# Relative-position attention and a sine-activated feed-forward on one core: bias bands from TensorE instead of a DRAM bounce, another load order, and a staged key transpose for the second batch

## The chip, the cores and the metric

The kernel runs on one NeuronCore of a Trainium2 chip. The metric is device time in microseconds (us) of one execution; before the change it is 374.09 us, the median of 3 runs (373.94 to 374.35).

## The reference

Eight batches, eight heads, 576 positions, head size 64. Attention with a bias that depends only on the distance of two positions, then a feed-forward with a sine:

```
scores = q @ k.T / 8 ; scores += bias_table[bucket(|i - j|)]     # 32 buckets, one value for each head
attn   = softmax(scores) ; x = attn @ v                          # x: 4608 x 512, heads side by side
h = x @ w_in ; g = h + sin(alpha*h)**2 / alpha ; out = g @ w_out # 512 -> 2048 -> 512
```

Every distance of 128 or more falls into the last bucket, so the bias differs from that bucket's value only in a band around the diagonal. The kernel subtracts the last bucket's value from the table (which softmax does not feel), takes the exponential of the rest, and multiplies the exponentials of the scores by this factor inside the band alone.

## The kernel before, in words

One Python planner (`Plan`, L61) holds some thousands of tasks, each with a cost, dependencies, a priority and an earliest time, and writes the instructions of all engines in one fixed order. The planner's times leave no trace in the program except through that order: each engine runs its own list from top to bottom and waits on semaphores.

Work goes by batch `t` (8 of them). For a batch: scores by TensorE (PE) in units of 128 keys x 512 queries x 2 heads into PSUM (L682 to L706), exponentials by ScalarE (ACT, L723), band multiplications by VectorE (DVE, L754), products with v on PE (`plan_av`, L973), a normalization on DVE (L967, L968), and a transpose into `xT`. The feed-forward of block `b` follows: `w_in` products (L1078), sine and some squares on ACT (L1083, L1090), other squares and the sum on DVE (L1092, L1097), and `w_out` products (L1139 to L1142) which the planner lays into gaps of PE's work, mostly during the next batch's attention. All matrix products come from the helper `full` at L478, so in the profile they share that line and are told apart by their tiles.

The first batch is loaded as fp32 or cast by the queue of GpSimd (POOL), and its keys and queries are transposed on PE, head pair by head pair (`plan_tr`, L564, matmuls at L573 and L579), copied out of PSUM by DVE (L562). The second batch's keys and queries come in natural order too (tile `nat2`, `load_nat2`, L542) and are transposed on PE in the middle of block 0's feed-forward. From batch 2 on, POOL writes fp16 copies to DRAM (`staged_k`, `staged_q`, L405), and the queue of SyncE (SP) turns them on the way back with DMA transposes (L412). GpSimd copies the last 64 keys of each head into `kt` (L416, L599).

The band factors: the table difference is made with a matmul of `less_last` and the table `tabN` (L613), its exponential is `tabE` (L616); a product with the one-hot constant `phi_sb` spreads it over 512 distances (`e_sb`, L622, L625). It is written five times to DRAM (`e_dram`, L626) and read back by SP with a stride of one element from partition to partition, into `m2r` and `mhr` (L492, L499, L630 to L633). Six of the eight loads of the first batch's v (`load_v32`) stand behind these reads in SP's list.

POOL's queue in the first 50 us: natural-order keys and queries of batch 0, casts of v, `w_in` in three pieces (L459), `nat2` keys then queries (L454), `w_out` in four pieces (L464), v of batch 1 (L424, L448), then the staging of batch 2 (L407). PE's fillers (`warm1`, L484, tile `zz`) are matmuls without a use that the planner writes where it sees a gap in the first 26 us.

`HEAD_PRI` (L255) is a table by hand or search: it gives the priorities of the first tasks by number.

Of the kernel before, what the change touches and what calls it, by code (L numbers as in the profile page):

```python
# [10 lines left out]
F16 = mybir.dt.float16  # L11
# [26 lines left out]
BANKS = {"h": (0, 1, 2, 3, 4, 5), "av": (6, 7), "mo": (7, 6)}  # L38

# [21 lines left out]
class Plan:  # L61
# [86 lines left out]
    def run(self, t0):  # L148
        free = dict(t0)
        todo = list(self.tasks)  # L150
        while todo:
# [21 lines left out]
            for e, c in cands.items():  # L173
# [5 lines left out]
                fin = st + t.engs[e]  # L179
# [34 lines left out]
T_START = {"PE": 4.25, "ACT": 5.2, "DVE": 5.05, "POOL": 5.5, "SP": 5.0}  # L214
SPLIT = {0: 3, 1: 3}
PRI_S = 0
T_WI = 16.4
T_TAB = 4.9
T_PHI = 5.4
T_CL = 9.6  # L220
T_FIRST = (4.3, 5.35)
T_PAIR = ((7.05, 8.1), (8.9, 10.6), (12.5, 13.4))
PRI_TR = (350, 950, 1250)
T_VT = 9.7
T_ACT = ()
T_M2 = (12.4, 14.6, 16.0, 16.0)
T_MH = 13.5
T_RST = 20.0
T_WL = 25.0
T_V0 = (6.5, 8.8, 16.4, 16.9, 17.4, 17.9, 18.4, 18.9)  # L230
T_P3 = 8.3
# [5 lines left out]
T_LD = 33.0  # L237
# [4 lines left out]
SQ = {"ACT": 0.52, "DVE": 0.38}  # L242
T_V = ((15.0, 15.0), (53.5, 53.5))
T_TR1 = (35.5, 39.0)
T_W = (24.2, 27.0, 33.0, 33.0)
T_WO = (42.0, 45.0, 47.8, 51.0)
WARM0 = 7
WARM1 = 0
# [18 lines left out]
}  # L267
SIN_SET = "trig_and_small"
SLACK = {"PE": 0.02, "ACT": 0.02, "DVE": 0.02, "POOL": 0.02, "SP": 0.02}
# [14 lines left out]
def kernel(  # L284
# [26 lines left out]
    NE = 5  # L311
# [8 lines left out]
    e_dram = nc.dram_tensor("e_dram", [NE, 4 * H, EW], F16, kind="Internal")  # L320
# [5 lines left out]
    last_np = np.eye(NB, dtype=np.float32)  # L326
    last_np[NB - 1] -= 1.0
    phi_h = nc.inline_tensor(phi_np, "phi_const")
    last_h = nc.inline_tensor(last_np, "last_const")
# [8 lines left out]
    m2r = sgl.tile([128, H, XW], F16, name="m2r")  # L338
    mhr = sgl.tile([128, NP, 192], F16, name="mhr")
    m2 = m2r[:, :, ::-1]  # L340
    mh = mhr[:, :, ::-1]
# [12 lines left out]
    tabN = sgl.tile([NB, H], F32, name="tabN")  # L354
    tabE = sgl.tile([NB, H], F16, name="tabE")
    phi_sb = sgl.tile([NB, EW], F16, name="phi_sb")
    less_last = sgl.tile([NB, NB], F32, name="less_last")
    e_sb = sgl.tile([H, EW], F16, name="e_sb")
    alphaN = sgl.tile([NF, 128], F32, name="alphaN")
    idf_sb = sgl.tile([NF, NF], F32, name="idf_sb")  # L360
# [886 lines left out]
```

## Time and profile before

| | |
|---|---|
| median of the runs | 374.09 us |
| profiled execution, first to last instruction | 372.5 us |
| what the runs' median has beside that span | 1.6 us |
| PE, ACT, DVE, POOL busy | 363.7, 318.3, 258.8, 89.2 us |
| start of the first score exponential | 9.39 us |
| start of the long stretch of `w_in` products of block 0 | 31.19 us |
| first score product of batch 1 | 51.49 us |

The profile gives only the span of the profiled execution, not a separate time for it. PE's busy time counts matmuls from issue to their modelled end, so neighbours overlap, and a stretch with full busy time need not be at the highest rate. "PEclk" is the granted clock of TensorE. An engine's list is in order, so one waiting instruction holds all behind it.

### The profile page before, as it was taken

The numbers are of one execution on the slowest core, as the hardware profiler recorded it, in microseconds if no ns is written. First come the engines' busy times: TensorE is split into PE (matmuls) and PEld (weight loads), VectorE is DVE, ScalarE is ACT, GpSimd is POOL, SyncE is SP. The second block draws the span as 40 slices with busy tenths as digits, with TensorE's granted clock in tenths as the row PEclk, the third lists the DMA queues.
The fourth block names the chain that finished last, engine by engine and source line by source line (L and its number), as shares of the span: only waits on it lengthen the run. The fifth ranks groups of instructions, "written<-read, shape, count | busy, mean of one in ns | idle before, by whom it ended". The sixth has DMA issues, their size and how long they took to land.

```text
span 372.5 us, 8907 instructions
## 1 busy us (share of the span) xinstructions
PE 363.7 (98%) x3563; PEld 195.3 (52%) x3563; DVE 258.8 (69%) x555; ACT 318.3 (85%) x436; POOL 89.2 (24%) x130
## 2 busy tenths in 40 slices
PE   6989989999999999999999999999999999999996
PEld 2455445644465445784554456444676455444443
DVE  4697966678776967597659866787669675879100
ACT  2898999989998999799989999899979997999211
POOL 5575360065000730064003700090006000000000
PEclk9599999999999999999999999999999999999999
DMA  9799999299824996199917992699249121000122
GB/s 167 152 191 208 203 170 155 61 146 123 113 60 99 115 151 112 48 161 138 135 48 135 126 169 59 115 114 171 60 111 118 65 58 48 7 18 13 59 85 84
DMA packets 149690, 40.69 MB, mean 109 GB/s; under 512 B 137144, under 2 KB 144656, under 8 KB 149648
## 3 DMA queue, kind: packets, MB, share of 16 engines
q0 software_dynamic: 94928, 17.47, 58.1%
q1 hardware_dynamic: 54352, 22.30, 25.5%
q8 instruction: 28, 0.46, 0.5%
q10 hardware_dynamic: 368, 0.34, 0.3%
q14 instruction: 14, 0.11, 0.1%
HBM read 37.73 MB, written 16.56 MB: 146 GB/s over the span
## 4 chain that ended last, share of the span: by engine, by line
PE 87%; DVE 4%; DMA 3%; ACT 3%; issue 1%; SPq 0%; ACTq 0%; DVEq 0%
PE pb L478 86%; DVE g L1097 1%; DMA tabN<-in_bias_table_dram 1%; DVE u L754 1%; DMA m2r<-e_dram 1%; DMA e_dram<-e_sb 1%; ACT sq L1090 1%; PE pb L1039 1%; ACT s L1083 1%; ACT nat L723 1%; DVE sq L1092 0%; DVE kT L562 0%; ACT L1161 0%; SPq L501 0%; DVE xn L968 0%
## 5 line engine op out<-in xcount | busy, mean ns | idle before, releaser
L723 ACT ACTIVATE u<-pb 128x1024 f16<-128x1024 f32 (+1 forms) x146 | 137.6, 1015 | 8.8 <-PE pb L478 7.4
L478 PE MATMUL pb<-w_out,g 128*128 128x512 f16 (+2 forms) x592 | 138.7, 374 | 0.5 <-DVE kT L562 0.5
L478 PE MATMUL pb<-xT,w_in 128*128 128x512 f16 (+4 forms) x704 | 127.5, 340 | 0.0
L1097 DVE SCALAR_TENSOR_TENSOR g<-sq,inv_a,pb 128x512 f16<-128x512 f16 x144 | 101.1, 743 | 7.7 <-ACT sq L1090 3.8
L1083 ACT ACTIVATE s<-pb,alphaT 128x512 f16<-128x512 f32 x144 | 92.9, 692 | 11.1 <-PE pb L478 10.2
L478 PEld LDWEIGHTS <-w_in 128*128 128x128 f16 x704 | 64.6, 98 | 57.1
L754 DVE TENSOR_TENSOR u<-u,m2r 128x768 f16<-128x768 f16 (+1 forms) x128 | 63.2, 498 | 35.6 <-ACT u L723 33.7
L478 PEld LDWEIGHTS <-g 128*128 128x128 f16 x592 | 54.0, 98 | 60.3 <-issue 5.4
L478 PEld LDWEIGHTS <-u 128*128 128x128 f16 x1152 | 43.1, 97 | 10.9 <-issue 5.8
L1090 ACT ACTIVATE sq<-s 128x512 f16<-128x512 f16 x75 | 46.8, 637 | 1.2 <-DVE g L1097 0.3
L419 POOL COPY kt<-kT 64x256 f16<-64x256 f16 x12 | 5.1, 428 | 174.2 <-DMA kT<-staged_k 144.9
L478 PE MATMUL pb<-qT,kT 64*128 64x64 f16 (+1 forms) x512 | 44.0, 293 | 1.6 <-ACT u L723 0.6
L478 PE MATMUL pb<-v,u 128*128 128x65 f16 x1024 | 43.7, 193 | 0.0
L1092 DVE TENSOR_TENSOR sq<-s 128x512 f16<-128x512 f16 x69 | 28.8, 427 | 12.1 <-ACT s L1083 11.2
L968 DVE TENSOR_TENSOR xn<-pb,rd 128x256 f16<-128x256 f32 (+2 forms) x59 | 28.5, 483 | 2.0
L478 PEld LDWEIGHTS <-kT 64*128 64x128 f16 x512 | 16.3, 95 | 23.1 <-issue 16.2
L478 PE MATMUL pb<-vh,u 128*128 128x130 f16 x128 | 28.3, 221 | 0.0
L424 POOL DMA_DIRECT2D v<-in_v_dram x28 | 24.8, 898 | 6.9 <-DMA w_in<-in_moe_w_in_dram 2.6
L560 ACT ACTIVATE outs<-pb 128x512 f32<-128x512 f32 (+2 forms) x10 | 5.5, 554 | 19.9 <-PE pb L478 19.9
L562 DVE COPY outs<-pb 128x512 f32<-128x512 f32 x27 | 18.5, 686 | 3.8 <-PE pb L478 3.8
L1161 ACT ACT_TABLE_LOAD x15 | 19.2, 1283 | 0.3
L967 DVE RECIPROCAL rd<-pb 128x4 f32<-128x4 f32 (+2 forms) x59 | 11.0, 186 | 10.8 <-PE pb L478 10.7
(74 smaller groups left out, 181.2 us busy)
## 6 DMA issues: line engine op xcount, KB each, us to landing
out_dram<-outs SPq DMA_DIRECT2D x35, 256.0 KB, 2.3
v<-in_v_dram POOLq DMA_DIRECT2D x28, 128.0 KB, 5.1
staged_k<-in_k_dram POOLq DMA_DIRECT2D x6, 576.0 KB, 9.6
staged_q<-in_q_dram POOLq DMA_DIRECT2D x6, 576.0 KB, 12.0
w_out<-in_moe_w_out_dram POOLq DMA_DIRECT2D x4, 512.0 KB, 17.4
w_out<-in_v_dram SPq DMA_DIRECT2D x8, 128.0 KB, 5.2
w_in<-in_moe_w_in_dram POOLq DMA_DIRECT2D x2, 512.0 KB, 6.3
w_in<-in_moe_w_in_dram POOLq DMA_DIRECT2D x1, 1024.0 KB, 11.6
```

The source lines that it names most:

```text
L424: nc.gpsimd.dma_start(out=vs[t % 2][:, c, :, 0:D], in_=vp[128 * c : 128 * c + 128],)
L478: nc.tensor.matmul(out=out, lhsT=lhsT, rhs=rhs, start=start, stop=stop)
L562: k_of(e).tensor_copy(out=o, in_=i)
L723: nc.scalar.activation(out=o, in_=x, func=AF.Exp, scale=0.125)
L754: nc.vector.tensor_tensor(out=io, in0=io, in1=m2[:, 2 * p : 2 * p + 2, x0 : x0 + hi - lo], op=ALU.mult)
L967: nc.vector.reciprocal(out=r, in_=x[:, :, :, D])
L968: nc.vector.tensor_tensor(out=xn[:, 0:n].rearrange("p c (z d) -> p c z d", z=2), in0=x[:, :, :, 0:D], in1=r.unsqueeze(3).to_broadcast([128 ...
L1083: nc.scalar.activation(out=s16.v, in_=h.v, func=AF.Sin, scale=alphaT[:, f : f + 1])
L1090: nc.scalar.activation(out=sq.v, in_=s16.v, func=AF.Square)
L1092: k_of(e).tensor_tensor(out=sq.v, in0=s16.v, in1=s16.v, op=ALU.mult)
L1097: nc.vector.scalar_tensor_tensor(out=gcell[b].v[:, f, :], in0=sq.v, scalar=inv_a[:, f : f + 1], in1=h.v, op0=ALU.mult, op1=ALU.add,)
L1161: nc.scalar.preload_act_table_set(name)
```

## The change

It has five parts.

1. **Bands on TensorE.** `phi` becomes a 128 x 512 constant: four copies of the one-hot table, each shifted by one distance, and four mask columns. `less_last` (now made on DVE from an identity) gives the table on all four partition groups; DVE spreads it into `tab4` (32 columns: head by shift). For each third of a band, 32 matmuls with a sliding 128-column window of `phi_sb` as stationary operand and `tab4` as moving operand (128 x 32 each) fill two PSUM banks, and one copy by ACT or DVE puts 128 x 8 x 128 values into `m2`. `mh` is copied from `m2`. `e_sb`, `e_dram` and its reads go.
2. **Bias table first.** `tabN` is POOL's first DMA instead of ACT's fourth; `phi_sb` goes from SP's queue to ACT's.
3. **v of batch 0 and `w_in` earlier.** All eight v loads follow each other in SP's list; the `w_in` loads stand in POOL's list after the first v cast.
4. **Keys of batch 1 staged.** They are written to `staged_k` by POOL and turned by an SP DMA transpose; `kt` is copied from there by DVE. The queries still come as `nat2` and over PE.
5. **New order.** The planner gets a DMA "engine" with sizes for each load, a slower PE between two times (`COLD`), other costs, and 250 new entries of `HEAD_PRI`. Tasks of block 0 depend on modelled loads instead of fixed times.

Cut to its core:

```diff
-LAT = {"PE": 0.2, "ACT": 0.18, "DVE": 0.18, "POOL": 0.2, "SP": 2.4}
+LAT = {"PE": 0.2, "ACT": 0.18, "DVE": 0.18, "POOL": 0.2, "SP": 2.4, "DMA": 1.9}
...
+T_START = {"PE": 4.25, "ACT": 5.2, "DVE": 5.05, "POOL": 6.7, "SP": 9.0, "DMA": 13.3}
+STAGED = (0,)
+COLD = (8.4, 14.0, 1.2)
 HEAD_PRI = {
+    0: 5620.10946, 1: 10120.37866, 2: 5619.629986, 3: 10068.1594, 4: 10068.68213, 5: 5620.024503, 6: 5620.936454, 7: 10068.51148, 8: 5619.947209, 9: 10069.00727,
...
-    phi_np = np.zeros((NB, EW), dtype=np.float16)
-    for x in range(EW - 1):
-        phi_np[bt[abs(x - 255)], x] = 1.0
+    phi_np = np.zeros((NJ * NB, EW), dtype=np.float16)
+    for j in range(NJ):
+        for x in range(EW - NJ):
+            phi_np[NB * j + bt[abs(x - 252 - j)], x] = 1.0
+        phi_np[NB * j : NB * j + NB, EW - NJ + j] = 1.0
...
+    def stage(t, kq):
+        dst, src = ((staged_k, k), (staged_q, q))[kq]
+        nc.gpsimd.dma_start(
+            out=dst.ap()[t].rearrange("s (h d) -> s h d", h=H),
+            in_=src[t].rearrange("h s d -> s h d"),
+        )
...
+    P_.dma_start(out=tabN, in_=bias_table)
     P_.memset(id_sb, 1.0)
...
-    nc.scalar.dma_start(out=less_last, in_=last_h.ap())
-    nc.scalar.dma_start(out=tabN, in_=bias_table)
-    nc.sync.dma_start(out=phi_sb, in_=phi_h.ap())
+    nc.scalar.dma_start(out=phi_sb, in_=phi_h.ap())
     nc.sync.dma_start(out=alphaN, in_=moe_alpha.rearrange("(f p) -> f p", p=128))
     load_v32(0)
     load_v32(1)
     load_vt32()
+    for h in range(2, H):
+        load_v32(h)
...
+        def spread(e):
+            nc.vector.tensor_tensor(
+                out=tab4, in0=tabE.unsqueeze(2).to_broadcast([NJ * NB, H, NJ]),
+                in1=phi_sb[:, EW - NJ : EW].unsqueeze(1).to_broadcast([NJ * NB, H, NJ]), op=ALU.mult,
+            )
...
+        tab = plan.add({"DVE": 0.12}, spread, [x], -3000, nb=T_PHI)
+        n = XW // 3
+        for k, w in enumerate((1, 2, 0)):
+            b = Buf("sc")
+            def mm(e, b=b, w=w):
+                o = bank(b, 2).rearrange("p k x -> p (k x)")
+                for i in range(n // NJ):
+                    x0 = EW - NJ - 128 - n * w - NJ * i
+                    full(o[:, NJ * H * i : NJ * H * (i + 1)], phi_sb[:, x0 : x0 + 128],
+                         tab4.rearrange("p h j -> p (h j)"), True, True)
+            def cp(e, b=b, w=w):
+                copy_on(e, m2[:, :, n * w : n * (w + 1)].rearrange("p h (i j) -> p h i j", j=NJ),
+                        bank(b, 2).rearrange("p k x -> p (k x)").rearrange("p (i h j) -> p h i j", h=H, j=NJ))
+            x = plan.add({"PE": BAND_PE}, mm, [tab], -1100 + 10 * k, new=[b])
+            bands[w] = plan.add({"ACT": 0.95, "DVE": 1.15}, cp, [x], -1100 + 10 * k, use=[b])
...
+    def load(eng, cost, emit, size, pri, deps=(), after=(), nb=0.0):
+        x = plan.add({eng: cost}, lambda e: emit(), deps, pri, nb, after=after)
...
+        return x, plan.add({"DMA": size}, lambda e: None, [y], pri)
...
+        for kq in range(2):
+            if kq in STAGED:
+                pool("kq%d" % kq, (2.3, 2.6)[kq], lambda kq=kq: stage(1, kq), (4.4, 5.0)[kq])
+            else:
+                pool("kq%d" % kq, 0.8, lambda kq=kq: load_nat2(kq), 3.1)
...
-                for kq in range(2):
-                    tr[(1, p, kq)] = plan_tr(1, p, kq, 10085 + 20 * p, T_TR1[kq])
+            for kq in range(2):
+                y = [loads["%s%d" % ("t" if kq in STAGED else "kq", kq)][1]]
+                if kq in STAGED:
+                    z = []
+                    if kq == 0:
+                        z = [plan.add({"DVE": 0.35}, lambda e: load_kt(1, nc.vector), y, 10080)]
+                    for p in range(NP):
+                        tr[(1, p, kq)] = y, z
+                    continue
+                for p in range(NP):
+                    tr[(1, p, kq)] = plan_tr(1, p, kq, 10085 + 20 * p, 0.0, y)
```

The change moves instructions at three places that matter below.

POOL's list around the loads of batch 1 and of the weights, before (`w_in`, `nat` with buffer 95 is `nat2`):

```order
L459 DMA w_in_78<-in_moe_w_in_dram 128x4x1024
L740 TENSOR_TENSOR u<-u,mhr 128x128
L444 CAST v_72<-w_out_79 128x4x64 x3
L454 DMA nat_95<-in_k_dram 96x8x384
L454 DMA nat_95<-in_q_dram 96x8x384
L740 TENSOR_TENSOR u<-u,mhr 128x128
L464 DMA w_out_79<-in_moe_w_out_dram 128x4x512 x4
L424 DMA v_73<-in_v_dram 128x8x64 x4
L448 DMA vh_75<-in_v_dram 64x4x64 x2
```

The same place after the change (the last `w_in` load stands 12 rows above the first row):

```order
L809 TENSOR_TENSOR u<-u,mh 128x128
L616 COPY kt_70<-kT_66 64x64 x2
L422 DMA staged_k<-in_k_dram 4608x1x64
L616 COPY kt_70<-kT_66 64x64 x2
L482 DMA nat_95<-in_q_dram 96x8x384
L809 TENSOR_TENSOR u<-u,mh 128x128
L491 DMA w_out_79<-in_moe_w_out_dram 128x4x512 x3
L809 TENSOR_TENSOR u<-u,mh 128x128
L491 DMA w_out_79<-in_moe_w_out_dram 128x4x512
L448 DMA v_73<-in_v_dram 128x8x64 x4
```

The staging of batch 1's keys now stands between `w_in` and the `nat2` queries, in the same queue.

PE's list where block 0's `w_in` products become dense, before (`xn` is the normalized attention output, turned into `xT`):

```order
L478 MATMUL pb<-xT,w_in_78 128x512
L1039 LDWEIGHTS xn
L1039 MATMUL pb<-id_sb,xn 128x128
...
L478 LDWEIGHTS w_in_78
L478 MATMUL pb<-xT,w_in_78 128x512
```

The same place after:

```order
L505 MATMUL pb<-xT,w_in_78 128x512
L593 LDWEIGHTS nat_95
L593 MATMUL pb<-id_sb,nat_95 64x96
...
L1109 LDWEIGHTS xn
L1109 MATMUL pb<-id_sb,xn 128x128
...
L593 LDWEIGHTS nat_95
L593 MATMUL pb<-id_sb,nat_95 64x96
...
L505 LDWEIGHTS w_in_78
L505 MATMUL pb<-xT,w_in_78 128x512
```

Two of the four transposes of batch 1's queries (12 matmuls each) have moved from between the dense products to ahead of them, one of them ahead of the last turn of `xn`.

ACT's list at the start of the score exponentials, before (`u` holds exponentials of scores):

```order
L616 ACTIVATE tabE<-pb 32x8
L625 ACTIVATE e_sb<-pb 8x512
L626 DMA e_dram<-e_sb 8x5x512
L723 ACTIVATE u<-pb 128x2x512 x3
L723 ACTIVATE u<-pb 128x512
```

After (`m_76` is the band table `m2`):

```order
L630 ACTIVATE tabE<-pb 128x8
L574 ACTIVATE m_76<-pb 128x8x128
L791 ACTIVATE u<-pb 128x2x512 x3
L791 ACTIVATE u<-pb 128x512
L791 ACTIVATE u<-pb 128x2x512
L574 ACTIVATE m_76<-pb 128x8x128
```

Two band copies stand in ACT's list where `e_sb` stood; the third is on DVE.

More of the change, by code (lines that the diff above doesn't have):

```diff
@@ L241 @@
 NORM0 = 1200
[L242 to L246, printed above, removed]
+SQ = {"ACT": 0.53, "DVE": 0.41}
 WARM0 = 7
+COLD = (8.4, 14.0, 1.2)
 WARM1 = 0
@@ L310 @@
     EW = 512
-    NE = 5
+    NJ = 4
     ctx.enter_context(tc.manual_schedule())
@@ L512 @@
     )
+    P_.tensor_copy(out=idf_sb, in_=id_sb[0:NB, 0:NB])
     for kq, src in ((0, k), (1, q)):
@@ L608, in plan_table @@
     def plan_table():
-        a, b = Buf("h"), Buf("h")
+        a = Buf("h")
         def less(e):
-            full(bank(a)[0:NB, 0:H], less_last, tabN, True, True)
+            full(bank(a)[:, 0:H], less_last.rearrange("a j b -> a (j b)"), tabN, True, True)
         def ex(e):
-            nc.scalar.activation(out=tabE, in_=bank(a)[0:NB, 0:H], func=AF.Exp)
-        x = plan.add({"PE": 0.15}, less, [], -1200, nb=T_TAB, new=[a])
-        x = plan.add({"ACT": 0.15}, ex, [x], -1200, use=[a])
-        def mm(e):
-            full(bank(b)[0:H, 0:EW], tabE, phi_sb, True, True)
@@ L742, in bd @@
                 )
-            d = plan.add({"POOL": 0.6} if t == 0 and p else {"DVE": 0.25 if two else 0.15}, bd, [x],
-                         base + 10, nb=late, use=[ub])
+            d = plan.add({"POOL": 0.6} if t == 0 and p else {"DVE": 0.25 if two else 0.15}, bd, [x] + band,
+                         base + 10, use=[ub])
             for pp in (p, p + 1) if two else (p,):
```

229 lines of the change are left out of this document (120 added, 109 removed), and 35 rows, old and new, of the table HEAD_PRI.

## Prediction

> **What bounds the kernel now.** I read the page's busy times and its chain first.
>
> ```profile
> PE 363.7 (98%) x3563; PEld 195.3 (52%) x3563; DVE 258.8 (69%) x555; ACT 318.3 (85%) x436; POOL 89.2 (24%) x130
> PE 87%; DVE 4%; DMA 3%; ACT 3%; issue 1%; SPq 0%; ACTq 0%; DVEq 0%
> ```
>
> TensorE is busy 98% of the span and holds 87% of the chain. The chain in order of time and the busy times by stretch tell where it does not:
>
> ```profile
> 2.22 4.77 DMA tabN<-in_bias_table_dram
> ...
> 8.81 3.42 DMA e_dram<-e_sb
> ...
> 13.96 4.43 DMA m2r<-e_dram
> ...
> 75.86 37.92 PE pb L478 x358
> 60.00:360.00 300.00, 300.00 (x2891) 161.96 (x2890) 215.35 (x457) 266.03 (x361) 57.22 (x64) 1.00 0.78 96
> ```
>
> In the first 20 us the chain hangs on the bias table's load, the bounce and the read back. From 60 to 360 us PE has no idle time. So a change early in the program counts only by how much sooner PE comes to its long dense work, and by what PE no longer has to do after that. PE's timeline around that point (start, length, operation, idle before):
>
> ```profile
> 30.32 0.28 PE L1039 MATMUL pb<-id_sb,xn 128*128 128x128 f16 x2
> ...
> 31.19 8.36 PE L478 MATMUL pb<-xT,w_in 128*128 128x512 f16 x38
> 39.48 0.70 PE L579 MATMUL pb<-id_sb,nat 96*64 96x96 f16 x24
> 40.12 1.90 PE L478 MATMUL pb<-xT,w_in 128*128 128x512 f16 x8
> 41.95 0.45 PE L579 MATMUL pb<-id_sb,nat 96*64 96x96 f16 x12
> 42.33 1.04 PE L478 MATMUL pb<-xT,w_in 128*128 128x512 f16 x4
> ...
> 47.00 0.45 PE L579 MATMUL pb<-id_sb,nat 96*64 96x96 f16 x12 [0.31 <-ACT qT L560]
> 47.91 0.59 PE L478 MATMUL pb<-w_out,g 128*128 128x512 f16 x2 [0.47 <-DVE kT L562]
> ...
> 52.40 0.67 PE L478 MATMUL pb<-qT,kT 64*128 64x512 f16 x4 [0.52 <-ACT nat L723]
> ```
>
> I call the start of the 38 products P; it is 31.19. Behind P, PE works to the end with only three short waits, 0.31 + 0.47 + 0.52 = 1.30 us.
>
> **The work behind P.** Of the eight transposes of batch 1, the four of the keys go away (a DMA turns them) and two of the queries move ahead of P, so six of 12 matmuls leave this stretch. By the starts above 12 take 42.33 - 41.95 = 0.38 and 24 take 40.12 - 39.48 = 0.64; at 0.37 each, six are 2.2 us. The waits of 0.31 and 0.47 end with copies of kT and qT on ACT and DVE, of which half are gone. The remaining copies and the squares still keep both engines nearly as full as PE, so I leave 0.5 of the 1.30 us and count 0.8 gained; the bounds are 0 and 1.3. The `w_out` products only change places: 13 more of them come ahead of batch 1's first score product and as many fewer after. So, if P' is the new P, the span is P' + (372.5 - 31.19) - 2.2 - 0.8 = P' + 338.3.
>
> **The head up to the end of batch 0's attention.** Its parts, with the half-clock stretch, are in these rows (PE, ACT, and the granted clock as the third number from the end in the stretches):
>
> ```profile
> 7.12 0.20 PE L478 MATMUL pb<-tabN,less_last 32*32 32x8 f32 x2 [1.94 <-DMA tabN<-in_bias_table_dram]
> 9.28 0.69 PE L579 MATMUL pb<-id_sb,nat 96*64 96x96 f16 x12
> 9.90 0.61 PE L478 MATMUL pb<-qT,kT 64*128 64x512 f16 x2
> ...
> 9.39 2.18 ACT L723 ACTIVATE u<-pb 128x1024 f16<-128x1024 f32 x2 [0.61 <-PE pb L478]
> 24.68 1.03 ACT L723 ACTIVATE u<-pb 128x1024 f16<-128x1024 f32 x1
> 26.30 2.43 ACT L723 ACTIVATE u<-pb 128x1024 f16<-128x1024 f32 x3 [0.59 <-PE pb L478]
> 5.17 0.76 DVE L562 COPY kT<-pb 128x576 f16<-128x576 f16 x1
> ...
> 8.00:8.50 0.50, 0.50 (x7) 0.42 (x6) 0.50 (x1) 0.31 (x1) 0.00 (x0) 0.73 1.22 233
> 18.50:19.00 0.50, 0.50 (x5) 0.19 (x3) 0.50 (x1) 0.50 (x1) 0.37 (x1) 1.00 1.20 313
> ```
>
> The 1.94 us in which PE waited for the bias table, with the first query transposes queued behind it, go away. The band needs 96 matmuls of 32 columns, which the trace does not show. The nearest rows are 12 transposes of 96 columns: 0.38/12 = 32 ns at full clock, (9.90 - 9.28)/12 = 52 ns at half clock. Below lies zero; I take the two rows, 1.0 or 1.65 us for 32. ACT gets two band copies of the exponential's shape (1024 elements from PSUM, 1.03 us in the row) and loses `e_sb`. The first copy must precede the first exponential. With `tab4` at about 6.5 (an estimate: behind the key copy on DVE, which ends at 5.93, and the load of `phi`, four times larger than before), band matmuls to 7.6 and the copy to about 8.75, the first exponential comes at 8.75 instead of 9.39. Then ACT pays a second copy (1.0) and waits about 2 us for bands two and three on PE at half clock, against 0.61 + 0.59 and some smaller waits before. The exponentials ended at 26.30 + 2.43 = 28.73; mine end at 28.8, between 27.2 (clock never falls) and 30. DVE gains the band tables 3 to 10 us earlier, and pays about 2 us for a cast and two copies in time where it was idle. So **the attention of batch 0 ends about when it did**, and PE could take up the dense products at about 31.5, between 30 and 32.7.
>
> **The load that comes last.** Ahead of them PE now has the `nat2` query transposes. When do the queries land? First, the order in which POOL's queue finishes. POOL's own timeline shows it, since it waits for old transfers before it issues more:
>
> ```profile
> 25.32 0.83 POOL L454 DMA_DIRECT2D nat<-in_k_dram  x1
> 35.02 0.88 POOL L424 DMA_DIRECT2D v<-in_v_dram  x1 [2.64 <-DMA w_in<-in_moe_w_in_dram]
> 38.00 0.87 POOL L424 DMA_DIRECT2D v<-in_v_dram  x1 [2.10 <-DMA nat<-in_k_dram]
> 40.84 0.87 POOL L424 DMA_DIRECT2D v<-in_v_dram  x1 [1.97 <-DMA nat<-in_q_dram]
> 43.36 0.63 POOL L448 DMA_DIRECT2D vh<-in_v_dram  x1 [1.65 <-DMA w_out<-in_moe_w_out_dram]
> ```
>
> `w_in`, keys, queries, `w_out` end in the order of issue, each about 2.6 to 3 us after the one before. After the change `staged_k` stands ahead of the queries, so they land behind it. Rates, by stretch (the last number is GB/s), and the sizes of one transfer, with its time to landing:
>
> ```profile
> 12.00:12.50 0.50, 0.50 (x10) 0.24 (x6) 0.16 (x1) 0.50 (x1) 0.26 (x1) 0.50 0.00 0
> 30.00:40.00 10.00, 10.00 (x72) 4.76 (x69) 7.67 (x16) 9.00 (x16) 4.14 (x6) 1.00 1.25 206
> 91.00:91.50 0.50, 0.50 (x4) 0.24 (x3) 0.50 (x2) 0.50 (x1) 0.00 (x0) 1.00 2.43 155
> ...
> staged_k<-in_k_dram POOLq DMA_DIRECT2D x6, 576.0 KB, 9.6
> w_out<-in_v_dram SPq DMA_DIRECT2D x8, 128.0 KB, 5.2
> w_in<-in_moe_w_in_dram POOLq DMA_DIRECT2D x1, 1024.0 KB, 11.6
> phi_sb<-phi_const SPq DMA_DIRECT2D x1, 32.0 KB, 3.5
> ```
>
> At 12.0 all that was issued early had moved; the queue was empty. The changed program moves the same by then, and further, without a pause: six more v loads (6 x 131 KB at about 270 GB/s, an estimate under the 313 of the stretch at 18.50, when v was what moved: 2.9 us), three more quarters of `phi` (98 KB, 0.4), `w_in` (2.1 MB at 206 GB/s, 10.2), `staged_k` (590 KB at 155, the rate of the staging at 91 us: 3.8), the queries (590 KB at 206: 2.9). That is 20.2 us, so 32.2; the queue is not full just before 12.0 (0.8 less) and landing takes some tenths (0.8 more). POOL issues `staged_k` at about 20, behind a copy of batch 0's keys, which is well before `w_in` has moved. I take 32.2, with 30.5 (all at the best rates) and 34.5 (the key transposes take their share, below) as ends. This is later than the 30.3 at which PE gets there: **PE waits about 2 us for the queries**, with the last `xn` turn and all of block 0's products queued behind. Then come two transposes and a turn, 0.37 + 0.11 + 0.37, and a hand-over of 0.1: P' = 33.2.
>
> **Sum.** 33.2 + 338.3 = 371.5 span; with the 1.6 us that the median of the runs has beside the profiled span, **373.1 us**, 1.0 below 374.1. What the head wins or loses by about 1 us is hidden by the wait; if the wait goes, the end of the attention is next (31.5), and the full gain appears.
>
> **Two rules of the Trainium skill** bear on this wait. A PE gap of 1.94 us was followed by half clock from about 8.2 to 18.5 in the rows above, and the seven `zz` matmuls of the start took 0.45 us each, twice the 0.22 of the 38 products:
>
> ```profile
> 1.27 3.17 PE L478 MATMUL pb<-zz 128*128 128x512 f16 x7 [1.27 <-DVE zz L532]
> ```
>
> The Trainium skill, "TensorE: Matmul & The Clock Gate", Part 1, has the half clock come after an idle window of about 3.4 us. By that, a wait of 2 us costs nothing more and the sum stays 373.1; the trace disagrees, since less idle time was enough, so a rival below carries it. The Trainium skill, "DMA: Bandwidth & Descriptors", Queues, rings and completion order, lets each DMA engine go round its queues packet by packet. By that, the turning of batch 1's keys on SP's queue, which starts when `staged_k` has landed, would take half of the engines from the queries, up to 1.4 us: 374.5. No row of before shows the two together.
>
> **Rivals.**
> - *No wait*: loads at their best rates, or the attention ends late enough. P' = 30.7 to 32.3, middle 31.6: 371.5. For it: the early stretch moved up to 313 GB/s. Against: the cast loads moved 206 GB/s in the row of 30 to 40 us. Chance 0.20.
> - *The wait trips the clock* (slower): as at 7.12, PE idles about 2 us, the granted clock halves, and the dense products take 0.43 instead of 0.22 each. The price is 1.6 us if the clock comes back after 3.2 us, as after the `zz` row, and up to 5 us if after 10 as in the mixed work of 8 to 18. Near the first: 374.7 to 376. It decides from a gap of about 1.9 us on. Against: work around this gap is denser than around the first. Chance 0.22.
> - *The head is later than the load*: `phi` lands late, or half-clock bands starve ACT; the attention ends 3 us later, P' = 34.6: 374.5 to 376. Chance 0.08.
> - *The change moves no bound*: the gain behind P is eaten by ACT and DVE, 374.1. Chance 0.05.
>
> **Numbers.** The forecast, 372.2 to 374.2 with 373.1 in its middle, has 0.45. A measurement of this kernel tells about 0.2% (0.75 us) from no change. Faster than that: two thirds of the forecast (0.30) and the first rival (0.20), 0.50. Within: 0.10 of the forecast, 0.05 of the clock's rival, 0.05 of the last, 0.20. Slower: 0.05, 0.17 and 0.08, 0.30. The range 370.4 to 376.2 leaves out the deepest case on each side.
>
> **What would show it.** In the new profile: PE's wait at the query transposes (`nat`), with the DMA of `nat` as releaser, of about 2 us; `staged_k` landing ahead of it at 29 to 30; dense products from 33; no waits on `m2`; the clock at 1.00 behind the wait. If the transposes start without a wait, the DMA sum is wrong; if the exponentials end after 31, the head's sum is.

## The result, and the profile after

The changed kernel takes **383.81 us** (median of 4 runs, 383.74 to 383.93) beside 374.01 us for the kernel before on the same chip: a ratio of 1.0244, 95% interval 1.0207 to 1.0282. It is 9.8 us slower. The forecast was 373.1 us, between 370.4 and 376.2: a small gain, where there is a clear loss.

The profiled execution has a span of 382.1 us, 9.6 more than before. The page's busy times, PE's busy tenths in 40 equal slices of the span, and the granted clock in the same slices:

```profile
PE 364.3 (95%) x3607; PEld 196.8 (51%) x3607; DVE 260.1 (68%) x563; ACT 316.2 (83%) x432; POOL 89.0 (23%) x123
...
PE   8539999999999999999999999999999999999996
...
PEclk9858999999999999999999999999999999999999
```

PE has as much to do as before (364.3 against 363.7 us) and does it in 95% of the span instead of 98%. So the loss is idle time. The row of PE puts it into slices 2 and 3, about 10 to 29 us, and the clock is low there and in slice 4. PE's own timeline (start, length, operation, idle time before it and what ended it):

```profile
6.57 0.95 PE L505 MATMUL pb<-tab,phi_sb 128*128 128x32 f16 x32
...
17.70 0.61 PE L505 MATMUL pb<-qT,kt 128*128 128x256 f16 x2 [3.92 <-POOL kt L616]
27.55 0.60 PE L505 MATMUL pb<-v,u 128*128 128x65 f16 x8 [6.14 <-POOL v L472]
40.88 0.45 PE L593 MATMUL pb<-id_sb,nat 96*64 96x96 f16 x12 [0.50 <-DMA nat<-in_q_dram]
41.85 4.06 PE L505 MATMUL pb<-xT,w_in 128*128 128x512 f16 x18
```

The dense `w_in` products start at 41.85 instead of 31.19: that is 10.66 us, more than the whole loss. Ahead of them PE waits 3.92 us for a `kt` copy and 6.14 us for a cast of v, both on POOL. The wait for the queries, on which the prediction turned, is 0.50 us. POOL's timeline shows why the copy and the cast were late:

```profile
7.86 2.25 POOL L487 DMA_DIRECT2D w_in<-in_moe_w_in_dram  x3
...
16.42 0.56 POOL L472 CAST v<-w_out 128x256 f16<-128x256 f32 x1 [2.73 <-DMA w_out<-in_v_dram]
16.93 0.71 POOL L616 COPY kt<-kT 64x64 f16<-64x64 f16 x2
19.95 0.40 POOL L472 CAST v<-w_out 128x256 f16<-128x256 f32 x1 [2.31 <-DMA w_out<-in_v_dram]
25.45 0.40 POOL L472 CAST v<-w_out 128x256 f16<-128x256 f32 x1 [5.10 <-DMA w_out<-in_v_dram]
26.41 1.09 POOL L472 CAST v<-w_out 128x256 f16<-128x256 f32 x3 [0.56 <-DMA w_out<-in_v_dram]
...
28.31 2.21 POOL L422 DMA_DIRECT2D staged_k<-in_k_dram  x1
31.02 0.79 POOL L482 DMA_DIRECT2D nat<-in_q_dram  x1
```

Read it from top to bottom, since POOL works its list in order. The casts wait for the fp32 loads of v (tile `w_out`, where they are parked). Behind each cast stands what PE needs: the copy of `kt` at 16.93, which ends the 3.92 us; the cast of head 0, last of all, which ends the 6.14 us, since the first product with v needs heads 0 and 1; and then the staged keys at 28.31 and the queries at 31.02. The loads of v were issued by 10.8 us, and this is how long they took (the line of the v loads, all eight; the `w_in` loads below it):

```profile
DMA to landing us min/median/max: 3.9/8.3/16.5
...
w_in<-in_moe_w_in_dram POOLq DMA_DIRECT2D x2, 512.0 KB, 10.5
w_in<-in_moe_w_in_dram POOLq DMA_DIRECT2D x1, 1024.0 KB, 16.8
```

Before, the slowest v load took 6.1 us. Now it takes 16.5: it runs beside 2.1 MB of `w_in`. The busy times by stretch show what that does (PE first, then the granted clock, the DMA share and GB/s as the last three numbers):

```profile
15.00:20.00 5.00, 2.30 (x20) 1.06 (x21) 2.25 (x5) 1.67 (x3) 1.21 (x4) 0.54 1.21 199
20.00:25.00 5.00, 1.15 (x5) 0.24 (x3) 1.23 (x2) 2.36 (x3) 0.35 (x1) 0.50 1.08 197
25.00:30.00 5.00, 2.45 (x28) 1.79 (x28) 1.23 (x4) 0.71 (x1) 3.94 (x8) 0.50 0.03 5
30.00:35.00 5.00, 5.00 (x81) 3.71 (x78) 3.63 (x12) 4.16 (x7) 4.41 (x8) 0.75 1.49 96
```

From 15 to 25 the DMA engines are full and every compute engine is idle half of the time or more; from 25 to 30 the DMA engines have nothing to do (5 GB/s), because the next loads have not been issued: POOL, which issues them, has been waiting for the previous ones. PE works at half clock from about 18 to 32.

### The profile page after: what moved, and what is told of

Its sections match the earlier page's. It is cut to its first block, busy times and chain, and to the rows that moved or that the text cites. A ratio compares the mean times of both kernels' runs of the same rounds, so it can differ in the third digit from the quotient of the medians.

```text
span 382.1 us, 8960 instructions
## 1 busy us (share of the span) xinstructions
PE 364.3 (95%) x3607; PEld 196.8 (51%) x3607; DVE 260.1 (68%) x563; ACT 316.2 (83%) x432; POOL 89.0 (23%) x123
## 4 chain that ended last, share of the span: by engine, by line
PE 88%; DMA 8%; SPq 2%; ACT 1%; POOL 0%; DVE 0%; issue 0%; ACTq 0%; POOLq 0%
PE pb L505 87%; DMA w_out<-in_v_dram 4%; DMA nat<-in_q_dram 3%; SPq L459 1%; DMA natx<-in_k_dram 1%; ACT u L791 1%; PE pb L1109 0%; PE pb L593 0%; SPq L464 0%; POOL v L472 0%; DVE outs L576 0%; DVE u L823 0%; ACT xT L574 0%; ACT outs L574 0%; POOL kt L616 0%
## 5 line engine op out<-in xcount | busy, mean ns | idle before, releaser
L823 DVE TENSOR_TENSOR u<-u,m 128x768 f16<-128x768 f16 (+1 forms) x128 | 61.8, 489 | 34.0 <-ACT u L791 32.1
L505 PEld LDWEIGHTS <-u 128*128 128x128 f16 x1152 | 44.8, 99 | 17.1 <-issue 11.5
L505 PE MATMUL pb<-v,u 128*128 128x65 f16 x1024 | 45.2, 196 | 6.2 <-POOL v L472 6.1
L1160 ACT ACTIVATE sq<-s 128x512 f16<-128x512 f16 x80 | 49.5, 637 | 1.8 <-DVE g L1167 1.0
L505 PE MATMUL pb<-qT,kT 64*128 64x64 f16 (+1 forms) x512 | 42.4, 291 | 0.4 <-ACT u L791 0.3
L1162 DVE TENSOR_TENSOR sq<-s 128x512 f16<-128x512 f16 x64 | 26.9, 424 | 15.4 <-ACT s L1153 14.8
L505 PEld LDWEIGHTS <-kT 64*128 64x128 f16 x512 | 15.5, 95 | 22.9 <-issue 16.4
L576 DVE COPY outs<-pb 128x512 f32<-128x512 f32 x29 | 19.9, 687 | 2.2 <-PE pb L505 1.7
L574 ACT ACTIVATE outs<-pb 128x512 f32<-128x512 f32 (+2 forms) x8 | 4.3, 544 | 19.8 <-PE pb L505 19.8
```

The source lines that it names most:

```text
L505: nc.tensor.matmul(out=out, lhsT=lhsT, rhs=rhs, start=start, stop=stop)
L576: k_of(e).tensor_copy(out=o, in_=i)
L823: nc.vector.tensor_tensor(out=io, in0=io, in1=m2[:, 2 * p : 2 * p + 2, x0 : x0 + hi - lo], op=ALU.mult)
L1160: nc.scalar.activation(out=sq.v, in_=s16.v, func=AF.Square)
L1162: k_of(e).tensor_tensor(out=sq.v, in0=s16.v, in1=s16.v, op=ALU.mult)
```

## The experiments

Most of these kernels differ from the changed kernel, or from the one before, only in the place of a few steps on POOL. `e6`, `e7` and `e9` also give the planner new dependencies, `e12` and `e14` make one copy on another engine, and `e10` and `e13` turn the keys of batch 1 on TensorE, with new dependencies as well. The planner still makes its whole plan; a table `MOVED` then says behind which task others are written into the program. The common edit (`e1` to `e14`; it shifts line numbers by 7):

```diff
+MOVED = {17: [26, 28, 30]}
...
+        self.nth = list(self.tasks)
+        self.index = {t: i for i, t in enumerate(self.nth)}
...
-            t.emit(e)
+            i = self.index[t]
+            if not any(i in x for x in MOVED.values()):
+                t.emit(e)
+            for j in MOVED.get(i, ()):
+                self.nth[j].emit("POOL")
```

In the changed kernel tasks 17 to 24 are the casts of heads 0 to 7, 25 the clearing of the second set of buffers, 26, 28 and 30 the `w_in` loads, 32 the staged keys, 34 the queries, 67, 72 and 77 the `kt` copies for pairs 1 to 3. Theory A is the reading above: the early `w_in` loads delay v, and POOL's list passes the delay on. Rival B blames the staged keys ahead of the queries, rival C the order alone.

### w_in behind the casts

```diff
+MOVED = {17: [26, 28, 30]}
```

> The changed kernel, with its three `w_in` loads issued from GpSimd behind the last cast of `v` instead of ahead of them; every other instruction stands as it did. Theory A (the early `w_in` loads share the DMA engines with the six `v` loads and push their landing from about 15 to 26 us, and GpSimd's in-order list, held by the casts of `v`, passes the delay on to the `kt` copies, the products with v, the staged keys and the queries): the last `v` load lands by 18, the 3.92 us wait for `kt` is under 1 us, the dense stretch starts at 32 to 34, time 372 to 376. Rival B (the staged keys ahead of the queries in GpSimd's queue are the cost): the dense stretch still waits for the queries of the second batch beyond 38, time 379 to 383. Rival C (the order of GpSimd's list is the cost, whatever the DMA does): the waits behind the casts stay, time above 380.

Measured: **383.9 us**, ratio 1.0259 (1.0233 to 1.0284). No gain, though the first half of theory A held. The longest v load now takes 6.9 us, the casts of the eight heads wait 0.4 us in all, and the 3.92 us wait for `kt` is gone (a later `kt` copy costs 1.6 us, at 21.2); the last exponential of batch 0 ends at 28.6 us, where it ended before. Then (POOL, and PE's wait):

```profile
17.87 2.25 POOL L494 DMA_DIRECT2D w_in<-in_moe_w_in_dram  x3
...
24.05 0.79 POOL L489 DMA_DIRECT2D nat<-in_q_dram  x1
```

```profile
38.42 0.69 PE L600 MATMUL pb<-id_sb,nat 96*64 96x96 f16 x12 [7.44 <-DMA nat<-in_q_dram]
...
39.99 6.05 PE L512 MATMUL pb<-xT,w_in 128*128 128x512 f16 x18
```

and the stretch before:

```profile
15.00:20.00 5.00, 3.37 (x42) 1.66 (x42) 4.89 (x10) 5.00 (x7) 4.93 (x9) 1.00 0.11 9
```

The DMA engines stand idle from 15 to 20 us (9 GB/s), then get `w_in`, the staged keys and the queries together, and the queries, last in line, land at 38.4. They hold PE because their transposes stand ahead of the dense products. That wait is the one that rival B had named, though at 383.9 us instead of 379 to 383. So theory A was incomplete: what must be moved is the same either way, and the delay only changes its victim. During the wait the granted clock falls to 0.50, from 33.9 to about 44 us: the 18 products take 6.05 us instead of 4.06, 2.0 us more.

### The order of POOL's list alone

```diff
+MOVED = {32: [34, 17, 20, 19, 21, 22, 23, 24]}
```

> The changed kernel, `w_in` early as it is, but in GpSimd's list the copies of `kt` for pairs 1 and 2, the staged keys and the queries of the second batch stand ahead of the seven waiting casts of `v`. Theory A: `v` still lands at 26 or later, the wait for `kt` is gone, the exponentials of batch 0 end at about 29, but every product with v starts after 26, so the dense stretch starts at 34 to 37: 375 to 379. Rival B: the queries land by 26 and all of the loss is back, 373 to 375. Rival C: all of it is back too, 373 to 375, with no wait for v over 1 us.

Measured: **378.5 us**, ratio 1.0112 (1.0087 to 1.0137): 5.3 us of the 9.8 are back with `w_in` as early as it was.

```profile
22.78 0.60 PE L512 MATMUL pb<-v,u 128*128 128x65 f16 x8 [3.72 <-POOL v L479]
36.51 4.06 PE L512 MATMUL pb<-xT,w_in 128*128 128x512 f16 x18
```

The waits for `kt` and for the queries are gone. The products with v still start only at 22.78, behind the casts, and the last exponential ends at 33.2, 4.5 us late. Theory A's time (375 to 379) and its dense stretch (34 to 37) are met, but v landed somewhat sooner than the 26 that it named: the casts at 22.33 to 24.75 waited 0.8 us in all. Rivals B and C expected all of the loss back, and it is not. With v late, the order of the list is worth 5.3 us; the other 4.5 stay with the late v.

### The kernel before, with early w_in

Tasks 9 and 20 to 22 are here the last of the early key and query loads and the three `w_in` loads.

```diff
+MOVED = {9: [20, 21, 22]}
```

> The kernel before, with one edit: its three `w_in` loads are issued from GpSimd ahead of the waiting casts, right behind the loads of pair 3 (about 9 us instead of 15 to 18). It has no staged keys in the second batch, no bands on TensorE, and its own order. Theory A: the `v` loads, which it issues at 13 to 16 us, land at 24 or later, TensorE waits for v, the dense stretch starts at 37 to 41, 380 to 384 us. Rivals B and C (the staged keys, or the order of the changed kernel's list): no change, 374 plus or minus 0.7.

Measured: **381.4 us**, ratio 1.0193 (1.0165 to 1.0221): inside theory A's 380 to 384, in a kernel without any other part of the change (its `w_in` loads are issued from 8.1 us instead of 20.7). The victim is another one, though. The waits of PE and of DVE, up to 62 and 45 us, and a row of the landings:

```profile
PE pb L485 <- DVE kT L569: 5.4, 1, 5.4
```

```profile
DVE u L761 <- DMA m2r<-e_dram: 7.6, 2, 6.5
```

```profile
m2r<-e_dram SPq DMA_DIRECT2D x2, 192.0 KB, 9.3
```

Two of the three band reads take 9.3 us instead of 3.8, DVE waits 7.6 us for them, and PE for a key copy behind it in DVE's list. Rivals B and C, which expected no change, fall as the only cause. The dense stretch starts 7.1 us later, at 38.28. In this kernel, too, early `w_in` costs some 7 us, through what is loaded beside it.

### A quarter of w_in early

```diff
+MOVED = {17: [28, 30]}
```

> The changed kernel with only the first of its three `w_in` loads (a quarter of the bytes) issued early; the other two stand behind the last cast of `v`, as in the first run. Theory A (the bytes issued ahead set how late v lands): the last `v` load lands 2 to 4 us later than in the first run, not 11, and the casts run by 16 to 19 us; the queries land a little sooner than in the first run: the wait for them is 5 to 7 us, time 381 to 383.5. Rival (any early load on GpSimd's queue brings the whole delay): the casts wait until 24 us or later.

A single execution: 384.1 us (the kernel before had 375.1 on that chip). The longest v load takes 9.5 us, 2.6 more than with no `w_in` ahead; with all of it ahead it was 9.6 more. The last four casts run at 18.57 to 20.40, not at 24 or later: the delay goes with the bytes, not with the mere presence of a load. The time is that of the run with none of it early, above the expected 381 to 383.5: PE waited less for the queries (3.6 us), but 1.5 for v, and the clock was at half again (18 dense products in 6.34 us).

### The queries ahead of the staged keys; w_in in the middle

The first edit has `w_in` behind the casts and the queries first; the second has `w_in` behind the clearing, where all v loads are out, and the queries first.

```diff
+MOVED = {17: [26, 28, 30], 72: [34]}
```
```diff
+MOVED = {25: [26, 28, 30], 72: [34]}
```

> As the first of these runs (`w_in` behind the casts), and the queries of the second batch issued ahead of the staged keys. Theory A: the queries land 2 to 5 us sooner than in the first run, and the dense stretch starts up to 2 us sooner: 371 to 374. Rival B: this edit gives most of what comes back, 5 us or more below the first run.

> The changed kernel with two moves in GpSimd's list: the three `w_in` loads stand behind the clearing of the second set of buffers (about 13.4 us, when all `v` loads have been issued) and ahead of the waiting casts, and the queries of the second batch stand ahead of the staged keys. Theory A, as amended by the runs so far (the head is bound by what the DMA engines have to bring and by the order in which it is needed: v, then `w_in`, then the queries, whose transposes stand in TensorE's list ahead of the dense products): `v` lands by 17, the 6 us in which the DMA engines had nothing to do in the first run are used, the queries land at 30 to 33, TensorE waits 0 to 3 us for them, the dense stretch starts at 31 to 34, 372 to 375.5. Rival (staged keys, bands or the new order cost by themselves, wherever the loads stand): the dense stretch starts beyond 35, 376 or more.

Measured: **379.6 us** (1.0134, 1.0101 to 1.0168) and **375.5 us** (1.0006, 0.9978 to 1.0035). The first is 4.3 us below the run with the queries last, with a wait of 3.36 us for them instead of 7.44; the dense products start at 36.25 instead of 39.99, again at half clock (18 in 6.26 us). That is more than theory A allowed (up to 2) and less than rival B asked (5 or more), so with `w_in` late the place of the staged keys does cost. The second uses the 6 idle microseconds of the DMA engines: no wait for the queries at all, dense products from 34.44, and the loss is gone within the measurement. What it still waits for, in PE's list of waits:

```profile
PE pb L512 <- POOL kt L623: 3.0, 1, 3.0
```

### The transposes behind the dense products

To the edits of the second run above and of the first run, the planner gets one more line: the four groups of query transposes depend on the dense task 209.

```diff
+    for i in (185, 187, 189, 191):
+        plan.tasks[i].deps.append(plan.tasks[209])
```

> As the run with `w_in` in the middle and the queries first, and the four groups of query transposes of the second batch stand in TensorE's list behind the first 21 dense products instead of ahead of them. Amended theory A: no wait for the queries at all, the dense stretch starts at 29.5 to 31.5, 370 to 373; the next thing that can be late is the turned keys of the second batch, at about 50. Rival: as before, 376 or more.

> As the first run (`w_in` behind the last cast of `v`, staged keys ahead of the queries), with the query transposes behind the first 21 dense products. Amended theory A: the wait of 7.4 us for the queries, which was all that the first run lost, falls to 0 to 3 us, the dense stretch starts at 29.5 to 31.5, 370.5 to 374. Rival B (the staged keys ahead of the queries cost by themselves, through what they take of the DMA engines): the turned keys or the queries still hold TensorE by over 4 us, 376 or more.

Measured: **377.8 us** (1.0085, 1.0061 to 1.0110) and **383.5 us** (1.0207, 1.0140 to 1.0275). Both miss what I expected of theory A. No time is lost at the queries any more (0.3 and 1.3 us), and yet nothing is won. The chain of the first, in order of time:

```profile
33.77 16.69 DMA kT<-staged_k
50.46 0.02 issue
50.48 0.22 DVE kt L451
...
50.97 0.76 DVE g L1174
```

The next late load is the turned keys, which land at 50.46 and 55.48. They hold two `kt` copies in DVE's list, those hold a sum of `g`, and that holds PE's `w_out` products (1.0 and 2.0 us). In the first run this takes back nearly all that PE had won: it came to batch 1's first score product at 49.74 us, 1.09 sooner than without the edit. It does not explain why the time is worse. The new dependencies also change the planner's order in batch 1, and by batch 2's first product with v, with the same work done, PE is 0.65 us behind the run without the edit (93.98 against 93.33 us). In the second run the `w_in` loads were also issued 1.9 us later than in the first run (19.73), the clock was at half from about 17 to 26, and the turn of the keys ended 5 us later than in its twin; I have not separated these.

### The list in the order of need

```diff
+MOVED = {67: [26, 28, 30, 17, 19, 20], 72: [21, 22, 34, 23, 24, 32]}
```

> As the run with `w_in` in the middle and the queries ahead of the staged keys, and now GpSimd's list is ordered by when TensorE needs each step: the copy of `kt` for pair 1 ahead of `w_in` and of the casts, the cast of head 0 ahead of heads 2 to 7, the products of `mh` and the copy for pair 2 behind four casts. Theory A as amended: the 3.0 us wait for `kt` and the half clock that it brings at 15 to 25 us go, attention ends 2 to 4 us sooner, the dense stretch starts at 29 to 32, 371 to 374 against a kernel before of 374 to 375; the next limit is either the queries (landing at about 31) or the turned keys at about 50. Rival (bands on TensorE and the staged keys cost by themselves): no better than that earlier run, ratio 1.000 or more.

Measured: **374.5 us**, ratio 0.9990 (0.9964 to 1.0016). The dense stretch starts at 31.40, as expected, and the clock is granted in full through the head:

```profile
31.40 4.06 PE L512 MATMUL pb<-xT,w_in 128*128 128x512 f16 x18
```

The time is that of the kernel before, half a microsecond above what theory A expected, and the interval leaves room for its rival too (1.000 or more). Two variants follow: the staged keys ahead of four casts and of the queries, with the transposes behind (`e9`), and its twin in which TensorE turns the keys (`e10`, with `STAGED = ()`, priorities renumbered, and all eight groups of transposes behind 15 or more dense products).

```diff
+MOVED = {67: [26, 28, 30, 17, 19, 20], 72: [32, 21, 22, 23, 24, 34]}
```

> As the run with the copies ahead, but the staged keys are issued ahead of the last four casts and of the queries, and the query transposes stand behind 21 dense products. Theory A: the queries' later landing costs nothing, since they are needed only at about 36, and the turned keys land 2 to 4 us sooner, by about 48, so neither holds TensorE by over 1 us: 370.5 to 373.5. Rival (the staged keys and their turn hold the second batch wherever they stand, because the turn shares the DMA engines with `w_out` and the second batch's `v`): TensorE waits at 50 to 55 us behind the turned keys, 374 or more.

> The twin of the run with the keys first, without the staged keys: the second batch's keys are loaded like its queries and turned by TensorE (four more groups of 12 transposes, four copies out of PSUM and eight copies of `kt` on GpSimd), all behind 15 or more dense products. If the keys by DMA save what TensorE is spared (six groups of transposes at about 0.4 us in the prediction's count, here four), this run is 1.5 to 2.5 us slower than its twin. Rival B (the staged keys are what costs): this run is the faster one, by 1 us or more.

Measured: 377.9 us (1.0071, 1.0038 to 1.0105) and 379.1 us (1.0107, 1.0068 to 1.0145). Issuing the staged keys 2 us sooner brought the turned keys in at 50.46 instead of 50.89, 0.4 us. PE waits 2.0 us behind them, where it waited 0.9 without the new dependencies, and then works at half clock from 52.6 to 55.6 (seven `w_out` products in 3.17 us instead of 1.68): for that run its rival was right. The comparison with the twin is spoiled: in `e10` the products of `mh` came to stand behind the `w_out` loads on POOL, and PE waited 2.3 us for them. I draw nothing from it; the comparison is made again below.

The last improvement makes the `kt` copy of pair 3 on VectorE and moves VectorE's copies of the turned keys behind one product (task 184 behind 336):

```diff
+MOVED = {67: [26, 28, 30, 17, 19, 20], 72: [21, 22, 34, 23, 24, 32], 76: [77], 336: [184]}
...
-                k_of(e).tensor_copy(
+                k_of("DVE" if p == 3 else e).tensor_copy(
```

> The run with the copies ahead, with two more moves: the copy of `kt` for pair 3 is made on VectorE instead of GpSimd, where it stood behind the staged keys' issue, and VectorE's two copies of the second batch's `kt`, which wait for the turned keys, stand behind one product of `nat` with the bands. Theory A: the 1.6 us wait for `kt` in the head and half or more of the 0.9 us wait behind the turned keys go; the dense stretch starts at 29.8 to 30.8, but the turned keys, landing at about 50.5, then hold the second batch's first scores, so 0.5 to 1.5 us of it is kept: ratio 0.993 to 0.999. Rival (TensorE's idle time in the head is made up elsewhere): ratio 0.999 or more.

> The kernel with the last copy on VectorE once more, on the chip of the run without staged keys, for their difference: theory and rival as there; against the kernel before, a ratio between 0.995 and 1.002, as in its first run.

Measured: **374.45 us** (0.9998, 0.9973 to 1.0024) and, on another chip, **374.1 us** (0.9989, 0.9966 to 1.0012). Both waits that it was to remove are gone, and the time stays: the dense stretch starts at 31.85, not at 29.8 to 30.8, and its rival was nearer. In the first of the two, PE now waits for DVE instead (0.65 and 0.30 us for `xn`, 0.35 for `xT`). VectorE, which now makes the copy, is busy 4.83 of 5 us, where it was 3.83 without the move (third, fourth and fifth: DVE, ACT, POOL):

```profile
20.00:25.00 5.00, 3.91 (x70) 2.80 (x70) 4.83 (x14) 4.49 (x6) 5.00 (x8) 1.00 1.16 212
```

In the second, the same program, those waits are absent; the attention of batch 0 ends sooner, and PE waits 1.07 us for the queries. The dense stretch starts at 31.79 all the same.

No version beats the kernel before by more than can be measured; these are some 9 us better than the change as it was made.

### What the keys by DMA are worth

The same kernel, with the keys over TensorE and the products of `mh` ahead of `w_out` on POOL:

```diff
-STAGED = (0,)
+STAGED = ()
+MOVED = {65: [26, 28, 30, 17, 19, 20], 70: [21, 22, 34, 23, 24, 32], 74: [75], 138: [36, 38, 40], 150: [42, 44]}
```

> The last of the improved kernels (w_in in the middle, copies ahead, last copy on VectorE) without the staged keys: the second batch's keys come like its queries and are turned by TensorE behind 15 or more dense products; the products of mh stand ahead of the w_out loads on GpSimd. It differs from the kernel before in the bands made on TensorE, in the places of the loads and in the order. If the keys by DMA are worth what the prediction gave them (four of the six groups of transposes, about 1.4 us, and the waits behind their copies), this run is 1 to 2.5 us slower than the repeated run beside it. Rival: the staged keys give back what they save (their turn takes DMA time ahead of 50 us, TensorE or VectorE wait for it, and the end of the program comes later): this run is the same within 0.7 us or faster.

Measured: **376.2 us**, 1.0044 (1.0022 to 1.0066), beside 374.1 for the run with staged keys on the same chip: 2.1 us slower, as the theory said (1 to 2.5). This agrees with the price that the prediction gave the keys, and does not isolate it. In the profiled executions PE comes to batch 2's first product with v 4.3 us later (94.98 against 90.68 us), and four groups of transposes at 0.37 are 1.5 of that; the run also has new dependencies, which cost time in `e6` without touching the keys. Beside the kernel before, the interval lies above 1: bands on TensorE, the moved loads and the new order, without the staged keys, are slower in this form, not faster. The rival has one point that is real. ACT's last copy out of PSUM, in the kernel before, after the change, in this run and in its neighbour, with spans of 372.5, 382.1, 375.5 and 372.2:

```profile
369.69 0.28 ACT outs L560
```
```profile
378.42 0.28 ACT outs L574
```
```profile
372.65 0.28 ACT outs L581
```
```profile
368.35 0.28 ACT outs L581
```

From the end of that copy to the end of the span it is 2.5 us in the kernel before and 2.6 here, and 3.4 and 3.6 in the two with staged keys for batch 1. The other ten kernels with these staged keys have 3.4 to 3.7, and `e3` and `e10`, without them, 2.5 and 2.6. So they pay about 0.9 us more at the end. Why was not tried.

## Why the prediction was wrong, step by step

**The head up to the end of batch 0's attention** was the step that failed. The part that the trace of before could carry was right: 32 band matmuls took 0.95 us (I had 1.0 or 1.65), the wait for the table is gone, and the first exponential starts at 8.48 us (I had 8.75). The prediction put the end of the exponentials at 28.8, between 27.2 and 30; it was 38.0. "POOL issues `staged_k` at about 20" was the false sentence: it was 28.31. I had followed POOL's list only as a queue of loads. I had not gone through the casts and copies in it, nor asked when what they wait for would land. With the lists put right the sum holds: the exponentials end at 28.6 with late `w_in` and at 28.1 in `e8`.

**The load that comes last** failed with it, and in its method. I added up the bytes ahead of the queries, 20.2 us of transfer, and let v pass first. Two things were missing. Loads that are in flight together share the engines, so v paid for `w_in` (6.9 to 16.5 us at most, and 9.5 with a quarter of it). And the queue was not without a pause: 5 us of it were idle, because the engine that issues the next load was waiting for the last one. The queries landed at 40.8, not 32.2. The wait of 2 us was 0.50, since the attention was late by the same cause. The Trainium skill, "DMA: Bandwidth & Descriptors", Queues, rings and completion order, lets each DMA engine go round its queues packet by packet. The v loads on SP's queue, slowed by loads on POOL's, agree with that, with 16.5 against 6.9 us beside it. I had weighed the rule in the prediction for the turn of the keys, where it was worth 1.4 us; its place was here.

**The work behind P** was right up to batch 2, and wrong after it. The transposes of batch 1 behind the start of the dense products (PE's groups by shape, before and after):

```profile
L579 PE MATMUL pb<-id_sb,nat 96*64 96x96 f16 x96 | 3.2, 209 | 0.3 <-ACT qT L560 0.3
```
```profile
L593 PE MATMUL pb<-id_sb,nat 96*64 96x96 f16 x28 | 1.1, 209 | 0.0
```

That is 2.1 us less, where I had 2.2. I had P' + 338.3 for the span, and it was 382.1 - 41.85 = 340.25. Up to batch 2 the sum was a little short: from P to batch 2's first product with v it is 58.90 us, with four more `w_out` products (0.9 us) in it, instead of 61.54. That is 3.5 us less for the same work, where I had 3.0. What failed is that I took all that follows as unchanged. PE's first product with v of batch 2 and the `w_out` products at one place of that batch, before:

```profile
92.73 0.25 PE L478 MATMUL pb<-vh,nat 128*64 128x130 f16 x2
...
107.55 1.46 PE L478 MATMUL pb<-w_out,g 128*128 128x512 f16 x6
```

and after:

```profile
100.75 0.25 PE L505 MATMUL pb<-vh,nat 128*64 128x130 f16 x2
...
115.86 1.42 PE L505 MATMUL pb<-w_out,g 128*128 128x512 f16 x5
```

Six products take 1.46 us before, five take 1.42 after. In each of the batches 2 to 7, one `w_out` product starts 0.39 us behind the one before it, instead of 0.22; the kernel before has no such place. With a wait of 0.4 us for `outs`, PE needs 277.58 us from batch 2's first product with v to its last product, instead of 276.88, and for 0.9 us less work: 1.6 us lost. All the kernels made from the changed one have these 277.6 us, with staged keys for batch 1 and without, and `e3`, which has the old order, has 276.88. So neither the place of the loads nor the keys are the cause. The planner's new order is the likely one; no run changes it alone, and the profile does not name what holds that product. The end of the program, with the staged keys, adds 0.8 to 0.9 us.

This also answers why the repaired kernels do not reach the 371.5 us of the first rival, no wait. Their dense products start at 31.4 to 31.9, as early as that rival had them (30.7 to 32.3), but behind them stand 340.3 to 341.2 us, not 338.3. In `e12` PE comes to batch 2 at 90.75 us, 1.98 sooner than in the kernel before, and with more work done; the batches that follow and the end of the program take back all but 0.4 us of the span.

**The rivals.** Of the 0.30 that I gave to slower, 0.17 stood on the clock. "The head is later than the load" named the right place with two wrong causes (a late `phi`, half-clock bands), 3 us instead of 9, and had 0.08. The clock's price was near in size (1.6 us predicted, 2.0 measured in `e1`, behind a wait of 7.4 us), partly by luck: I had half clock for 3.2 us, read from the `zz` matmuls, for which the view gives a granted clock of 1.00, and in `e1` it stayed at half for 5.6 us after the queries had landed. And the wait of 0.50 us in the changed kernel did not bring it on: its 18 products took 4.06. The clock fell in the head, with the wait for `kt`; what that alone cost was not measured.

## What to carry to other kernels

When a load is issued earlier, list every transfer that is in flight at that time and ask which of them someone waits for; the cost falls on those, whichever queue they are on. Then go down the list of each engine that waits for them and note what stands behind the waiting instruction, loads that it issues above all: an engine that both waits for loads and issues loads turns one late transfer into idle DMA engines. And follow a gain to the next late load: here three were nested (v, the queries, the turned keys), and each repair brought the next to light. When the planner's order changes as well, compare the steady part too: 0.18 us in each of six batches, with the later end of the program, took back nearly all that the repaired head had won.

## What the runs showed of the hardware

The granted clock did not follow the length of a wait. In `e9` one PE wait of 0.94 us, ended at 14.77 us, was followed by a granted clock of 0.50 from 15 to 21; in `e8` PE idled 1.6 us ahead of 24.1 and the clock stayed at 1.00; in `e14` the clock fell to 0.50 from 18 to 21 behind three waits of 0.29 to 0.52 us. In `e12`, the same program as `e14`, and in `e8` the same three waits left it at 1.00. What decided is not shown. The Trainium skill, "TensorE: Matmul & The Clock Gate", Part 1, names an idle window of about 3.4 us; the first and the third of these fell after far less, and the second did not fall after more than the first.

The turn of 0.59 MB of staged keys took 16.7 to 19.0 us from issue to landing in the twelve kernels that have it (issued at 30 to 38 us), with `w_out` and the second batch's v in flight. Issuing the staging 2 us sooner (`e9` against `e8`) moved its end by 0.4 us.
